# A new timetable for the Fourier jobs in a fused Fourier-filter and MLP kernel

## The chip, the cores and the metric

The kernel runs on one core of a Trainium2 chip. The metric is device time in microseconds of one execution. Before the change it is 1558.96 us, the median of three runs (1558.42 to 1561.44). All data are 32-bit floats.

The core has a matrix engine (TensorE, in the profile PE, with its weight loads apart as PEld), three engines for elementwise work (VectorE as DVE, ScalarE as ACT, GpSimd as POOL), a queue engine (SyncE as SP), and 16 DMA engines that they share. DMA transfers are issued from SP, ACT and POOL, each in the order of its own instructions.

## The reference

Two blocks follow each other. The first is a filter in the Fourier space of the sequence, for eight sequences (batch) of 3136 rows and 256 channels:

```python
X = np.fft.rfft(x, axis=1)                      # x: (8, 3136, 256)
Y = X * (filt_r + 1j * filt_i)[None, :, :]
y = np.fft.irfft(Y, n=x.shape[1], axis=1)
```

The second takes the 25088 rows of the result as tokens:

```python
h = y.reshape(25088, 256) @ w_in                # 256 -> 1024
e = np.exp(h - h.max(-1, keepdims=True))
solu = h * (e / (e.sum(-1, keepdims=True) + 1e-9))
ln = (solu - mean(solu)) / np.sqrt(var(solu) + 1e-6) * g_ln
out = ln @ w_out                                # 1024 -> 256
```

## The kernel before

**Tokens.** The 25088 tokens are 196 blocks of 128. The main loop has 196 + 9 steps `k`; block k gets its hidden layer in step k, and later steps finish it. Two blocks form a pair, and a pair's work spans an even step and the odd one after it, so "pair j" below is steps 2j and 2j + 1. From pair 3 on each pair's first layer is seven products (line 875, tile `m`) instead of eight, in Strassen's manner, and its second layer seven projections (line 1022, tile `o`). The sums of operands that this needs are GpSimd's (line 854: four short ones of `y` for the first layer, and four of 128x512 each, tiles `u` and `solu_t`, for the second). ScalarE does the exponential (920), the square for the variance (940) and copies out of PSUM (896, 1038); VectorE the maxima (907, 910), the normalisation (932), a 32x32 block transpose (950) and the rest of the output (1042). SP regroups the transposed blocks by DMA (967, into `solu_t`) and stores the output (1050).

**Fourier jobs.** A sequence of 3136 = 49 x 64 rows is transformed in two stages with one trip through DRAM between them (`d1`), and back in two stages with another (`d2`). For each sequence e there are:

- 8 *first steps* (F): load rows of x on SP (line 273), a difference on VectorE (282) and a sum on GpSimd (288), eight matmuls of 49 rows (297, tile `pa`), two ScalarE copies (302), two stores to `d1` from the POOL queue (308).
- 7 *spectra* (S): load of `d1` (320) and of a table (835) from the ACT queue and of the filter (784) from the POOL queue, sixteen matmuls of 64 rows (330, tile `pb`), then the complex product on VectorE (353 to 355; line 355 is the addition of the two parts, with both inputs in SBUF). The seventh unit of a sequence is smaller than the other six.
- 7 *inverses* (I), always one step after their spectrum: sixteen matmuls of 64 rows (330, tile `pc`), two copies on ScalarE (406), a store to `d2` from the POOL queue (412), in the step after that.
- 8 *steps back* (B): two loads of `d2` from the POOL queue (421), 64 short matmuls of 50 rows (437, tile `py`), a ScalarE copy (442), two VectorE operations that write `y` (450, 451).

So F4 is a first step of sequence 4, and so on. The ordinary matmuls of the pair (875, 1022) use 128 rows; those of the four jobs use a half of the array's rows.

**What sets their places.** `PLAN` (line 41) has for each sequence e three lists of steps: of its first steps, of its spectra, and of its steps back. The loop at line 1066 puts each job's parts into lists by step: a spectrum at step t puts its matmuls into `early[t]`, its inverse into `late[t + 1]`, its stores into `stores[t + 2]`; a first step goes to `late[t]`; a step back to `early[t]` (a second one for the same step to `late[t]`). Function `step` (1146) runs these lists at fixed points among the pair's own operations: `early` after product 2 of an even step or products 5 of an odd one, `late` at the end of the step. In a step where both are planned, a step back's matmuls stand directly before the spectrum's, and an inverse's directly before the first step's:

```python
            for job in early[k]:          # line 1202
                job()
...
        for job in late[k] + loads[k]:    # line 1292
            job()
```

Loads of rows (for F, and of `d2` for B) have four buffers; line 1134 gives each load its step: three steps ahead of its use, or as soon as the load four places earlier has been used. The spectrum's loads are issued one pair ahead (lists `spectrum_loads` and `loads`). The order on every engine's queue is the order of the program; nothing is moved later.

Which jobs share a pair is thus a matter of `PLAN` alone. Before the change the plan of a sequence from e = 4 on repeats every 24 steps (12 pairs), and in steps 78 to 101, for example, pairs 39 and 40 have a step back each, 41 and 42 a step back, a spectrum and an inverse, 43 to 45 all four jobs, 46 and 47 all but a step back, 48 and 49 a first step, and pair 50 a first step and a step back.

Of the kernel before, what the change touches and what calls it, by code (L numbers as in the profile page):

```python
# [37 lines left out]
DIRECT = 3  # L38


PLAN = [
    None,
    ([0] * 6 + [1] * 2, [4, 5, 6, 7, 8, 10, 12], [16, 17, 18, 19, 20, 20, 21, 22]),
    ([3, 4, 5, 6, 7, 8, 9, 10], range(18, 32, 2), [34, 36, 38, 40, 42, 44, 46, 46]),
    ([15, 23, 25, 27, 29, 31, 33, 35], range(38, 52, 2), range(54, 70, 2)),
    (range(39, 55, 2), range(58, 72, 2), range(76, 92, 2)),
    (range(63, 79, 2), range(82, 96, 2), range(100, 116, 2)),
    (range(87, 103, 2), range(106, 120, 2), range(126, 142, 2)),
    (range(111, 127, 2), range(130, 144, 2), range(150, 166, 2)),
]  # L50
EPS_LN, EPS_SM = 1e-6, 1e-9

# [58 lines left out]
def kernel(  # L111
# [954 lines left out]
    for e in range(1, B):  # L1066
        first_at, spectrum_at, back_at = PLAN[e]
        sp = Spectrum(e, pools, load_filter, load_de)
# [269 lines left out]
```

## Time and profile before

| | |
|---|---|
| median of three runs | 1558.96 us |
| the profiled execution | 1558.44 us |
| its span, first to last instruction | 1556.7 us |
| PE, PEld busy | 1534.5 us (99%), 1066.0 us (68%) |
| DVE, POOL, ACT busy | 1241.3 us (80%), 1107.3 us (71%), 923.3 us (59%) |
| granted TensorE clock | 0.997 of full speed |
| DMA | 297.58 MB, mean 191 GB/s |

The columns of the profile: in the table of stages each row is a stretch of the span from:to in us, its length, then for each engine its busy time and the number of its instructions, the granted clock, the mean busy share of the 16 DMA engines and what they moved in GB/s. In the timeline each row is a start, a duration, an engine (PEld: a weight load), a line, an operation, the tile written and those read, shapes, and how many were merged into the row; in brackets stands how long the engine sat idle before it and what ended that. Matmuls are pipelined and their ends are modelled, so that the start of the next weight load says more than a matmul's end. A pair's start is here the start of its first product of line 875; there are fourteen matmuls of that line to a pair.

### The profile page before, as it was taken

What the parts mean: (1) busy time and instruction counts of PE and PEld (TensorE: products, weight loads), DVE (VectorE), ACT (ScalarE), POOL (GpSimd) and SP (SyncE); (2) the same over time, 40 slices, a digit from 0 to 9 for tenths busy, and PEclk for the clock granted to TensorE, in tenths of its full rate; (3) what the DMA queues carried; (4) which work ended last, traced back from release to release, by engine and by line L of the source; (5) the groups of instructions that cost most, each with busy time, mean ns of one, the idle gap of its engine ahead of it and who ended that gap; (6) DMA issues with size and microseconds to landing.
All of it is one profiled execution on the core that took longest, in us unless ns stands there. A gap on an engine that the chain in (4) does not pass through costs nothing. (4 is left out here: it accounts for less than half of the span.)

```text
span 1556.7 us, 36704 instructions
## 1 busy us (share of the span) xinstructions
PE 1534.5 (99%) x12922; PEld 1066.0 (68%) x12922; DVE 1241.3 (80%) x2220; ACT 923.3 (59%) x1893; POOL 1107.3 (71%) x1290
## 2 busy tenths in 40 slices
PE   9999999999999999999999999999999999999997
PEld 6735676666666776667666776667676777777777
DVE  5888878988988798868897699877987777777772
ACT  4556565665556565665656555665656656666662
POOL 2226776797879776986689678996767766676665
PEclk9999999999999999999999999999999999999999
DMA  9779587867986788667886678766874544344444
GB/s 250 267 254 274 160 229 218 238 196 212 245 242 188 188 247 238 198 164 202 248 230 183 166 209 246 209 181 185 228 206 118 135 122 121 97 119 105 107 109 109
DMA packets 340831, 297.58 MB, mean 191 GB/s; under 512 B 27313, under 2 KB 310731, under 8 KB 340649
## 3 DMA queue, kind: packets, MB, share of 16 engines
q1 hardware_dynamic: 277864, 175.33, 42.4%
q0 software_dynamic: 29152, 87.33, 18.7%
q10 hardware_dynamic: 33634, 32.58, 7.1%
q8 instruction: 105, 1.72, 0.5%
q14 instruction: 76, 0.62, 0.1%
HBM read 117.53 MB, written 74.84 MB: 124 GB/s over the span
## 5 line engine op out<-in xcount | busy, mean ns | idle before, releaser
L1022 PEld LDWEIGHTS o<-w_out_sb,solu_t 128*128 128x128 f32 x3136 | 381.7, 192 | 49.9 <-issue 43.1
L1022 PE MATMUL o<-w_out_sb,solu_t 128*128 128x128 f32 x3136 | 401.3, 276 | 3.7 <-DVE ot L1042 3.1
L1022 PEld LDWEIGHTS o<-w_out_sb,u 128*128 128x128 f32 x2352 | 307.3, 192 | 138.3 <-issue 108.6
L875 PE MATMUL m<-w_in_sb,s 128*128 128x512 f32 x760 | 384.5, 607 | 2.4 <-ACT h L896 1.6
L1022 PE MATMUL o<-w_out_sb,u 128*128 128x128 f32 x2352 | 310.7, 276 | 2.3 <-POOL u L854 1.8
L932 DVE SCALAR_TENSOR_TENSOR h<-e,h 128x1024 f32<-128x1024 f32 x196 | 304.5, 1554 | 0.0
L875 PE MATMUL m<-w_in_sb,y 128*128 128x512 f32 x570 | 297.1, 603 | 1.7 <-DVE h L907 1.2
L1038 ACT ACTIVATE ot<-o,rs_t 128x128 f32<-128x128 f32 x392 | 143.2, 367 | 244.6 <-PE o L1022 242.8
L896 ACT COPY h<-m 128x512 f32<-128x512 f32 x285 | 167.7, 588 | 200.5 <-PE m L875 179.7
L854 POOL TENSOR_TENSOR u<-solu_t 128x512 f32<-128x512 f32 x98 | 135.2, 1380 | 186.7 <-DMA solu_t<-turn 131.0
L910 DVE CUSTOM_DVE_ANT_0 h<-m,h 128x512 f32<-128x512 f32 x190 | 130.1, 685 | 166.8 <-ACT h L896 104.0
L940 ACT ACTIVATE h<-h,nmu 128x1024 f32<-128x1024 f32 x196 | 224.9, 1147 | 41.8 <-DVE turn L950 41.7
L950 DVE STREAM_TRANSPOSE turn<-h 128x1024 f32<-128x1024 f32 x196 | 243.2, 1241 | 3.2
L920 ACT ACTIVATE e<-h,nmax 128x1024 f32<-128x1024 f32 x196 | 225.3, 1149 | 9.3 <-DVE h L932 7.9
L854 POOL TENSOR_TENSOR u<-solu_t,u 128x512 f32<-128x512 f32 x98 | 136.9, 1396 | 99.6 <-PE o L1022 99.3
L1042 DVE SCALAR_TENSOR_TENSOR ot<-o,rs_t,ot 128x128 f32<-128x128 f32 x299 | 103.8, 347 | 100.1 <-ACT ot L1038 61.4
L875 PEld LDWEIGHTS m<-w_in_sb,s 128*128 128x128 f32 x760 | 124.5, 191 | 80.3 <-issue 63.0
L854 POOL TENSOR_TENSOR u<-u,solu_t 128x512 f32<-128x512 f32 x98 | 162.6, 1659 | 16.8 <-PE o L1022 7.6
L854 POOL TENSOR_TENSOR solu_t<-solu_t,solu_t 128x512 f32<-128x512 f32 x98 | 155.6, 1587 | 0.9
L875 PEld LDWEIGHTS m<-w_in_sb,y 128*128 128x128 f32 x570 | 93.6, 190 | 89.6 <-issue 45.9
L854 POOL TENSOR_TENSOR s<-y 128x128 f32<-128x128 f32 x190 | 94.4, 497 | 0.5
L437 PEld LDWEIGHTS py<-wb_t,t 50*64 50x64 f32 x3584 | 57.6, 134 | 42.9 <-issue 19.4
(153 smaller groups left out, 1939.0 us busy)
## 6 DMA issues: line engine op xcount, KB each, us to landing
solu_t<-turn SPq DMA_DIRECT2D x780, 128.0 KB
out_dram<-ot SPq DMA_DIRECT2D x196, 128.0 KB
t<-d POOLq DMA_DIRECT2D x112, 200.0 KB, 6.7
t<-d ACTq DMA_DIRECT2D x37, 512.0 KB
f<-f_dram POOLq DMA_DIRECT2D x37, 512.0 KB, 7.9
d<-g POOLq DMA_DIRECT2D x36, 512.0 KB, 4.8
d<-x POOLq DMA_DIRECT2D x80, 200.0 KB, 5.2
de<-de_tbl ACTq DMA_DIRECT2D x37, 256.0 KB
```

The source lines that it names most:

```text
L437: nc.tensor.matmul(out=views[g][64 * h:64 * h + 64, cb, i, :], lhsT=t4[rows, i, c0:c0 + 64], rhs=wb_t[rows, 0:N1], start=True, stop=True)
L854: nc.gpsimd.tensor_tensor(out=out, in0=in0, in1=in1, op=op)
L875: nc.tensor.matmul(out=ms[j, bank], lhsT=lhsT, rhs=w_in_sb[:, w, :], start=m in (1, 2, 7), stop=True, skip_group_check=True)
L896: nc.scalar.copy(out=h_half(k, i), in_=ms[j, 0])
L910: nc.vector.tensor_tensor_reduce(out=h_half(k, i), in0=ms[j, bank], in1=h_half(*kept), scale=1.0, scalar=sofar, op0=ALU.add, op1=ALU.min, ...
L920: nc.scalar.activation(out=e, in_=hs[k], func=AFT.Exp, bias=nmaxs.pop(k)[:, 1:2], scale=-1.0, accum_out=esums[g][:, i:i + 1])
L932: nc.vector.scalar_tensor_tensor(out=solu, in0=e, scalar=SHRINK, in1=solu, op0=ALU.mult, op1=ALU.mult, accum_out=nmu)
L940: nc.scalar.activation(out=solu, in_=solu, func=AFT.Square, bias=nmu, scale=-float(DFF), accum_out=variances[g][:, i:i + 1])
L950: nc.vector.transpose(out=turns[g][:, :, i, :], in_=solus[k].rearrange("p (f j) -> p f j", j=32))
L1022: nc.tensor.matmul(out=pos[p, bank], lhsT=lhs[:, f, :], rhs=w[:, f, :], start=f == 0 and (m in (1, 2, 7) or alone), stop=True, skip_group_ ...
L1038: nc.scalar.activation(out=out_half(p, *to)[0], in_=pos[p, 0], func=AFT.Copy, scale=rs)
L1042: nc.vector.scalar_tensor_tensor(out=ot, in0=pos[p, bank], scalar=rs, in1=out_half(p, *kept)[0], op0=ALU.mult, op1=ALU.add)
```

## The change

Only `PLAN` changes, with a small function that writes a list of seven steps with gaps. Spectra and steps back of a stretch of 24 steps from t now go to steps t, t+2, t+6, t+8, t+12, t+14, t+16 (and the eighth step back to t+18), and the first steps of the next sequence to the odd steps after those. From step 52 on the pattern of a stretch is: two pairs with all four jobs, one with none, two with all four, one with none, three with all four, one with a step back and a first step, two with none. In the stretch from 124 there is no sequence left for first steps. The steps before 52 are arranged anew as well: the spectra of sequence 2 begin at 14 instead of 18, the first steps of sequences 3 and 4 come earlier, the second step back that stood at 46 goes to step 35. Sequence 1 and the steps back of sequence 7 (150 to 164) stay where they were. No operation, tile or buffer is added or removed.

```diff
+def beside(t):
+
+    return [t + i for i in (0, 2, 6, 8, 12, 14, 16)]
+
+
 PLAN = [
     None,
     ([0] * 6 + [1] * 2, [4, 5, 6, 7, 8, 10, 12], [16, 17, 18, 19, 20, 20, 21, 22]),
-    ([3, 4, 5, 6, 7, 8, 9, 10], range(18, 32, 2), [34, 36, 38, 40, 42, 44, 46, 46]),
-    ([15, 23, 25, 27, 29, 31, 33, 35], range(38, 52, 2), range(54, 70, 2)),
-    (range(39, 55, 2), range(58, 72, 2), range(76, 92, 2)),
-    (range(63, 79, 2), range(82, 96, 2), range(100, 116, 2)),
-    (range(87, 103, 2), range(106, 120, 2), range(126, 142, 2)),
-    (range(111, 127, 2), range(130, 144, 2), range(150, 166, 2)),
+    ([3, 4, 5, 6, 7, 8, 9, 10], [14, 16, 22, 24, 26, 28, 30], [34, 35, 36, 38, 40, 42, 44, 46]),
+    ([13, 15, 17, 23, 25, 27, 29, 31], range(36, 50, 2), beside(52) + [70]),
+    (range(33, 49, 2), beside(52), beside(76) + [94]),
+    ([t + 1 for t in beside(52)] + [71], beside(76), beside(100) + [118]),
+    ([t + 1 for t in beside(76)] + [95], beside(100), beside(124) + [142]),
+    ([t + 1 for t in beside(100)] + [119], beside(124), range(150, 166, 2)),
 ]
```

## The prediction, made before the changed kernel ran

> **What bounds the kernel now.** I read the page first: shares, then chain. TensorE is busy all through, at full clock (0.997), and the chain that ended last goes through its products and projections.
>
> ```profile
> PE 1534.5 (99%) x12922; PEld 1066.0 (68%) x12922; DVE 1241.3 (80%) x2220; ACT 923.3 (59%) x1893; POOL 1107.3 (71%) x1290
> ...
> PE 38%; DMA 1%; POOL 0%; issue 0%; SPq 0%; ACTq 0%; DVE 0%; POOLq 0%; ACT 0%
> ```
>
> The change moves no operation into or out of the kernel, so an average over the span can't price it. I therefore cut the span at the starts of the pairs (each fourteenth matmul of line 875) and asked for busy times by stage. The rows are pairs 86 (no job), 76 (B), 48 (F), 50 (B and F), 54 (B, S, I), 46 (S, I, F), 32 (all four), 45 and 22 (all four); all have an even j except 45.
>
> ```profile
> core 0: us, PE busy (x) PEld busy (x) DVE busy (x) ACT busy (x) POOL busy (x), PEclk, DMA share, GB/s
> 1367.16:1379.64 12.48, 12.48 (x74) 9.13 (x73) 9.11 (x18) 7.70 (x17) 8.48 (x10) 1.00 0.44 118
> 1234.39:1248.15 13.76, 13.76 (x138) 10.08 (x137) 9.38 (x20) 8.20 (x18) 8.96 (x11) 1.00 0.52 142
> 824.25:837.93 13.68, 13.68 (x82) 9.40 (x80) 10.23 (x21) 8.93 (x19) 12.45 (x15) 1.00 0.64 176
> 851.40:866.36 14.96, 14.96 (x148) 10.35 (x144) 12.57 (x23) 9.43 (x20) 12.68 (x15) 1.00 0.68 172
> 909.37:925.31 15.94, 15.94 (x173) 11.30 (x169) 15.23 (x26) 9.51 (x20) 10.83 (x13) 1.00 0.81 236
> 793.75:809.57 15.82, 15.82 (x116) 10.60 (x112) 15.17 (x27) 10.00 (x23) 13.20 (x15) 1.00 0.76 215
> 576.46:593.25 16.79, 16.79 (x181) 11.62 (x177) 14.41 (x27) 10.26 (x22) 12.69 (x15) 1.00 0.90 259
> 775.88:793.75 17.87, 16.83 (x179) 11.47 (x175) 16.58 (x25) 9.68 (x21) 13.63 (x17) 1.00 0.83 232
> 418.89:437.49 18.60, 17.03 (x179) 11.69 (x177) 15.74 (x29) 10.77 (x25) 13.01 (x17) 1.00 0.97 268
> ```
>
> Seven rows have PE busy for the whole stretch: the pair takes what TensorE takes. The prices of the jobs follow by subtraction. B alone is 13.76 - 12.48 = 1.28, F alone 13.68 - 12.48 = 1.20, both in one pair 2.48: they add up, since one stands in the even step and the other at the end of the odd one. But with all four jobs, F costs 16.79 - 15.94 = **0.85** and B 16.79 - 15.82 = **0.97**. So F next to an inverse is 0.35 us cheaper, and B next to a spectrum 0.31. Spectrum and inverse have the rest, 16.79 - 12.48 - 0.85 - 0.97 = 2.49. (Odd pairs start from 12.27, without the small matmul that even ones have for the deviations; a sequence's last, smaller spectrum and inverse cost 13.82 - 12.27 = 1.55 in pair 71.) Why, the weight loads of pair 32 show:
>
> ```profile
> 578.20 0.30 PEld L875 LDWEIGHTS m<-w_in_sb,y 128*128 128x128 f32 x2
> 579.26 1.02 PEld L437 LDWEIGHTS py<-wb_t,t 50*64 50x64 f32 x64 [0.76 <-issue]
> 580.19 0.69 PEld L330 LDWEIGHTS pb<-t,de 64*64 64x64 f32 x16
> 581.27 0.30 PEld L875 LDWEIGHTS m<-w_in_sb,s 128*128 128x128 f32 x2 [0.39 <-issue]
> ```
>
> Going from 128-row matmuls to half-row ones opens a gap of 0.76 us in which no weights are loaded, going back one of 0.39 (0.82 after a first step); from `py` to `pb` there is none. Two neighbouring jobs share one way in and one way out.
>
> **The change by parts.** *Neighbours gained.* From the lists of the plan: F stands directly behind an inverse 5 + 7 + 5 + 5 + 5 = 27 times before (sequences 3 to 7) and 8 + 6 + 7 + 7 + 7 = 35 after; B directly ahead of a spectrum 3 + 5 + 6 + 5 + 5 + 6 = 30 times before (sequences 1 to 6) and 2 + 6 + 7 + 7 + 7 + 7 = 36 after. (The second B of step 46, now at 35, is alone in both.) That is 8 x 0.35 + 6 x 0.31 = **-4.7 us** on TensorE, on the path since nothing else ends these pairs. As a check I added such prices for every pair from 12 to 95: outside the pairs named next, and pair 14 (0.4 over), the sum meets the measured pair within 0.13 us.
>
> *Losses in full pairs.* Beyond its TensorE time, 16.57 (odd j) or 16.79 (even), a pair with all four jobs sometimes takes longer. The fifteen such pairs of before and their losses: pairs 19 to 23 0.6, 0, 0.8, 1.8, 0.6; 31 to 34 none; 43 to 45 0, 0, 1.3; 55 to 57 0.8, 0, 0. Together 5.9 us, 0.39 a pair. The new plan has 27 of them: 18 to 23, then seven in each of three stretches. Two causes are seen. In pair 45 a VectorE addition of two tiles in SBUF (line 355, median 0.855) ran 3.33 us while two GpSimd sums ran one behind the other, the output's VectorE operation came late, and the projection waited 1.23 us for its bank:
>
> ```profile
> 783.61 3.33 DVE L355 TENSOR_TENSOR pr<-pr,pt 128x512 f32<-128x512 f32 x1
> 783.88 1.27 POOL L854 TENSOR_TENSOR solu_t<-solu_t,solu_t 128x512 f32<-128x512 f32 x1
> 785.11 1.27 POOL L854 TENSOR_TENSOR u<-solu_t,u 128x512 f32<-128x512 f32 x1
> 787.25 0.97 PEld L1022 LDWEIGHTS o<-w_out_sb,solu_t 128*128 128x128 f32 x8 [1.23 <-DVE ot L1042]
> ```
>
> In pair 22, the fourth full one in a row, DMA is at 0.97 of its capacity, rows of x land late and ScalarE stands 4.25 us, partly behind its own DMA issues:
>
> ```profile
> 430.88 0.69 DVE L282 TENSOR_TENSOR diff<-x 113x512 f32<-113x512 f32 x1 [1.84 <-DMA x<-in_x_dram]
> 431.18 0.58 ACT L896 COPY h<-m 128x512 f32<-128x512 f32 x1 [4.25 <-DMA x<-in_x_dram]
> ```
>
> Bounds for the new losses: all gone, -5.9; or all 27 like pairs 19 to 23 (3.8 / 5 = 0.76), 27 x 0.76 - 5.9 = +14.6. I go by the place in a row of full pairs. First ones lost 1.4 in four, second ones 0 in four, third ones 2.1 in four, later ones 2.4 in three. The new plan has 10 firsts, 10 seconds, 4 thirds and 3 later ones: 3.6 + 0 + 2.1 + 2.4 = 8.1, so +2.2. But a first pair now follows an empty one, in which DMA is at 0.44 and GpSimd has no stores of earlier jobs to issue; half the firsts' loss is nearer. I take **+0.6**.
>
> *Other pairs.* Pairs 8 to 11 lost 0.1, 0.6, 1.4, 0.2 (pair 10 had two B in one step, S, a third B and I), 24 lost 0.9. The new pair 8 has B and S, then B, F and I: TensorE 18.1 us by the prices, VectorE some 17; no row shows this mix. Between no loss and pair 10's 1.4 I take 1.0, the mix being close to that one; pairs 9 and 10 have no spectrum any more, so 9 to 11 are put at 0.5 together; 24, left with a small S and I, at 0.1. That is 1.6 where 3.2 was, with bounds -3.2 (nothing lost) and +3.3 (8 to 11 at 1.4 each, 24 at its 0.9). Against these -1.6 I set one more loss like pair 22's 1.8 in the row 18 to 23, since pair 17 ahead of it now has two B and an F: **+0.2**.
>
> *What else moves with a job.* Each F takes along its loads on SP (among the regroupings of line 967), a VectorE difference (0.91), a GpSimd sum (1.29) and two stores on POOL (0.53 each); S two loads on the ACT queue, a load (0.75) and a store (0.78) on POOL, six VectorE operations (about 4.7 us), two ScalarE copies (0.56 each); B two POOL loads (0.54 each), a ScalarE copy (0.48), two VectorE operations (0.55 each). A full pair holds the same set before and after: VectorE 14.4 of 16.8 us, GpSimd 12.7, ScalarE 10.3. That cover is what hides them; where it fails is the loss above. Loads keep their lead in steps, but an empty pair is 12.4 us instead of 13.8: a spectrum's loads, issued 7 us into the pair before, have 9 us until the first `pb`, and pair 52's, landing 4 us after issue at a low DMA share, show room. Waits of the POOL queue on `d2` (B at 52, loaded at the end of the step that stores the last inverse) are as before at 54.
>
> Sum: -4.7 + 0.6 + 0.2 = -3.9. Against the profiled execution of 1558.44 (span 1556.7 and 1.7 around it; 0.5 below the median of the runs) this gives **1554.5 us**.
>
> **The rivals.**
> - *Loss by the number of full pairs* (VectorE and GpSimd in each other's way in each). At the old mean, 27 x 0.39 - 5.9 = +4.6 eats the gain: 1558.4. For: full pairs put the additions of line 355 beside the sums in each. Against: eleven of fifteen lost at most 0.6.
> - *Slower: every full pair like pairs 19 to 23*, through the same place, line 355 behind two GpSimd sums. 27 x 0.76 - 5.9 - 4.7 gives about +10: 1568.4. It decides above 0.51 a pair, (4.7 + 5.9 + 3.1) / 27, where 3.1 us is 0.2%, about what a measurement of this kernel can tell from no change. Against: pairs 31 to 34, four in a row without any loss.
> - *A longer first row.* Pairs 18 to 23 are six in a row behind a laden pair 17, where five lost 3.8, the last two 2.4 of it. DMA backlog adds two more such at 1.2 to 1.8, +3: about 1557.5.
> - *Empty pairs clear the queues*: the losses of the later stretches vanish (-2.1 instead of +0.6) and the first row gains a little: 1551.
>
> [...]
>
> **How the numbers follow.** My forecast has 0.45 (its own range 1552.5 to 1556.5), the empty-pair gain 0.10, the longer first row 0.10, loss by number 0.17, the slower rival 0.18. Faster by over 0.2% (under 1555.3) is most of the forecast, 0.38, and the gain: 0.48. Within 0.2%: 0.05 of the forecast, the first row, most of loss by number: 0.30. Slower: 0.22 with the tails. The range 1550.5 to 1562.5 leaves out the upper part of the slower rival and little below.
>
> **What would show it.** Pairs with all four jobs from 26 on at 16.57 and 16.79 us, empty ones at 12.27 and 12.48, pair 35 at 14.75; the same 0.76 gap, fewer of them (14 fewer ways in). Wrong if line 355 is long (over 2.5 us) in more than four or five full pairs, if empty pairs take over 12.6, since work left behind by a full pair holds TensorE there, or if spectra wait for `t`.

## The result, and the profile after

The changed kernel takes 1572.67 us (median of six runs, 1565.29 to 1576.64) against 1558.69 for the kernel before (six runs on the same chip, 1557.54 to 1563.36): a ratio over all runs of 1.0082 [1.0056, 1.0108] (the quotient of the two medians is 1.0090), so it is slower by 13 to 14 us where 4 us less were forecast. The profiled execution took 1572.86 us, its span 1571.1, at a granted clock of 0.998. (Line numbers of the changed kernel are 5 higher: 355 is now 360, 282 is 287, 437 is 442.)

The page of the changed kernel, engines and chain:

```profile
PE 1535.5 (98%) x12922; PEld 1065.1 (68%) x12922; DVE 1235.9 (79%) x2220; ACT 922.4 (59%) x1893; POOL 1098.0 (70%) x1290
...
PE 23%; DMA 1%; DVE 1%; issue 0%; POOL 0%; SPq 0%; ACT 0%; ACTq 0%; POOLq 0%; DVEq 0%
```

Busy shares have hardly moved; nothing in them tells of 14 us. The stages do. Cut at the pairs as before, the rows are pairs 86 (no job), 35 (B and F), 38 and 39 (a first and a second full pair), 40 (the empty one behind them), 26 (the first full pair of the new pattern), then 41, 42 and 43 (first full, second full, empty):

```profile
core 0: us, PE busy (x) PEld busy (x) DVE busy (x) ACT busy (x) POOL busy (x), PEclk, DMA share, GB/s
1382.90:1395.39 12.49, 12.49 (x74) 9.14 (x73) 8.88 (x18) 7.71 (x17) 8.55 (x10) 1.00 0.43 116
642.75:657.49 14.74, 14.74 (x144) 10.12 (x142) 10.87 (x21) 9.07 (x18) 11.23 (x15) 1.00 0.56 153
682.36:699.05 16.69, 16.69 (x178) 11.53 (x176) 14.72 (x27) 9.63 (x21) 10.76 (x10) 1.00 0.86 244
699.05:715.61 16.56, 16.56 (x178) 11.39 (x174) 14.82 (x27) 10.11 (x21) 16.12 (x18) 1.00 0.71 199
715.61:728.35 12.74, 12.74 (x77) 9.16 (x73) 10.97 (x18) 8.48 (x19) 10.26 (x14) 1.00 0.81 234
492.36:514.07 21.71, 18.71 (x179) 12.45 (x177) 14.95 (x27) 9.76 (x21) 10.11 (x11) 0.92 0.81 219
728.35:746.03 17.68, 17.68 (x176) 11.64 (x174) 15.71 (x25) 8.74 (x18) 11.99 (x14) 1.00 0.88 232
746.03:763.59 17.56, 17.56 (x179) 12.05 (x177) 15.87 (x27) 10.13 (x22) 15.00 (x16) 1.00 0.64 184
763.59:777.03 13.44, 12.87 (x72) 8.85 (x71) 9.72 (x20) 9.25 (x21) 9.33 (x14) 1.00 0.78 204
```

Two things stand in these rows. Where nothing is late, the pairs have the forecast lengths (16.69, 16.56, 14.74, 12.49). And the empty pair 40, between full ones, has DMA at 0.81, not at the 0.43 of an empty pair far from any job: the loads of the full pairs that follow are issued in it. In pairs 26 and 41 to 43 together 4.9 + 1.1 + 0.8 + 1.2 us are lost.

From here on the *loss* of a pair is its length less what the prediction's TensorE prices give for its jobs. Summed over pairs 4 to 96, the prices are 4.7 us lower after the change; the losses rise from 13.4 to 34.7 us, by 21.4 (21.35 before rounding); the stretches ahead of pair 4 and behind pair 96 are 2.3 us shorter: -4.7 + 21.4 - 2.3 = 14.4, which is the difference of the spans, 1571.1 - 1556.7.

Four kinds of place hold the new losses. The waits of VectorE's difference and of the steps back, after the change and before it (total us, times, longest):

```profile
DVE diff L287 <- DMA x<-in_x_dram: 21.2, 11, 3.3
...
PE py L442 <- DMA t<-d: 4.6, 4, 2.5
...
PEld py L442 <- DMA t<-d: 4.0, 2, 3.3
```

```profile
DVE diff L282 <- DMA x<-in_x_dram: 3.0, 4, 1.8
```

In the timeline of the changed kernel they look like this (pair 26, pair 29, pair 57):

```profile
497.63 0.20 PEld L442 LDWEIGHTS py<-wb_t,t 50*64 50x64 f32 x4 [3.32 <-DMA t<-d]
...
553.25 0.58 ACT L901 COPY h<-m 128x512 f32<-128x512 f32 x1 [2.90 <-DMA x<-in_x_dram]
553.61 1.64 DVE L287 TENSOR_TENSOR diff<-x 113x512 f32<-113x512 f32 x1 [2.23 <-DMA x<-in_x_dram]
...
987.13 0.69 DVE L287 TENSOR_TENSOR diff<-x 113x512 f32<-113x512 f32 x1 [3.30 <-DMA x<-in_x_dram]
988.49 0.30 PEld L880 LDWEIGHTS m<-w_in_sb,y 128*128 128x128 f32 x2 [3.16 <-DVE nmax L915]
```

(1) In pair 26 the first step back waits for its own load. (2) In pairs 20, 29, 32 and 57 the difference stands at the head of VectorE's queue without its rows; behind it are the maxima, and in pair 57 TensorE's next product waits until they are read (the last row). (3) In the second of two full pairs, 30 and again 42, VectorE's addition of the imaginary part is long, and the inverse's products of that part (tile `pc` from `pi`) have to wait for it:

```profile
574.74 2.50 DVE L360 TENSOR_TENSOR pi<-pi,pt 128x512 f32<-128x512 f32 x1
575.40 1.28 POOL L859 TENSOR_TENSOR u<-solu_t 128x512 f32<-128x512 f32 x1
...
576.50 0.63 PEld L335 LDWEIGHTS pc<-pr,de 64*64 64x64 f32 x8
...
576.76 1.62 POOL L859 TENSOR_TENSOR u<-u,solu_t 128x512 f32<-128x512 f32 x1
...
577.29 0.20 PEld L335 LDWEIGHTS pc<-pi,de 64*64 64x64 f32 x4 [0.16 <-DVE pi L360]
...
579.17 0.30 PEld L880 LDWEIGHTS m<-w_in_sb,y 128*128 128x128 f32 x2 [0.82 <-DVE h L912]
```

In a pair without loss, here 38, the weights of the two parts are loaded by turns:

```profile
697.15 0.14 PEld L335 LDWEIGHTS pc<-pr,de 64*64 64x64 f32 x2
697.18 0.14 PEld L335 LDWEIGHTS pc<-pi,de 64*64 64x64 f32 x2
```

In pair 30 the eight loads of the real part go first and alone. From the inverse's first weight load to the start of the next pair it takes 1.91 us in pair 38 and 2.67 in pair 30, and that is the pair's loss; the gap of 0.82 in the last row is the ordinary one behind a first step. This meeting costs 0.77 us in the full pair and 1.18 in the empty one, the same within 0.02 us in both places; pair 63 (B, S and I) loses 1.29 beside an addition of 2.26 us.

The first full pairs 29 and 41 have a meeting too. The difference has waited for its rows, so GpSimd's sum of the same rows falls beside the addition of the imaginary part (2.33 us in both pairs); the stretch from the inverse to the next pair is 2.86 us there, 0.95 over pair 38's. A late transfer and a long addition are thus not always two separate causes:

```profile
557.36 2.33 DVE L360 TENSOR_TENSOR pi<-pi,pt 128x512 f32<-128x512 f32 x1
...
557.85 1.27 POOL L293 TENSOR_TENSOR x<-x 113x512 f32<-113x512 f32 x1
```

(4) The rows of sequences 2 and 3, pairs 4 to 25, lose 16.0 us where they lost 10.9; 1.6 of the difference is in pair 4, whose plan is the same in both.

### The profile page after: what moved, and what is told of

It reads as the page before. It is cut to its first block, busy times and chain, and to the rows that moved or that the text cites. A ratio compares the mean times of both kernels' runs of the same rounds, so it can differ in the third digit from the quotient of the medians.

```text
span 1571.1 us, 36679 instructions
## 1 busy us (share of the span) xinstructions
PE 1535.5 (98%) x12922; PEld 1065.1 (68%) x12922; DVE 1235.9 (79%) x2220; ACT 922.4 (59%) x1893; POOL 1098.0 (70%) x1290
## 3 DMA queue, kind: packets, MB, share of 16 engines
q0 software_dynamic: 29152, 87.33, 18.4%
## 5 line engine op out<-in xcount | busy, mean ns | idle before, releaser
L937 DVE SCALAR_TENSOR_TENSOR h<-e,h 128x1024 f32<-128x1024 f32 x196 | 291.7, 1488 | 0.0
L859 POOL TENSOR_TENSOR u<-solu_t 128x512 f32<-128x512 f32 x98 | 131.5, 1341 | 194.3 <-DMA solu_t<-turn 102.2
L859 POOL TENSOR_TENSOR u<-u,solu_t 128x512 f32<-128x512 f32 x98 | 157.4, 1606 | 18.8 <-PE o L1027 12.5
L442 PEld LDWEIGHTS py<-wb_t,t 50*64 50x64 f32 x3584 | 58.4, 134 | 48.6 <-PE o L1027 14.4
```

The source lines that it names most:

```text
L442: nc.tensor.matmul(out=views[g][64 * h:64 * h + 64, cb, i, :], lhsT=t4[rows, i, c0:c0 + 64], rhs=wb_t[rows, 0:N1], start=True, stop=True)
L859: nc.gpsimd.tensor_tensor(out=out, in0=in0, in1=in1, op=op)
L937: nc.vector.scalar_tensor_tensor(out=solu, in0=e, scalar=SHRINK, in1=solu, op0=ALU.mult, op1=ALU.mult, accum_out=nmu)
```

## The experiments

Two theories stood against each other. *Transfers*: rows and tables land later than their lead allows, and VectorE, which is 14.7 to 15.9 us busy in the full pairs shown above, can't make up for it. *VectorE*: its additions of line 360, lengthened beside GpSimd's sums, are the loss, and the transfers are only what is seen in front. Each kernel was compared with the kernel before on the same chip, whose median there was 1558.97, 1560.95, 1560.84, 1560.89 and 1560.65 us; so ratios are compared, not times.

**Transfers left out of the new plan**

```diff
 def load_filter(sp, u, ...):        # and load_de in the same way
+    if sp.e > 3 or sp.e == 3 and u > 1:
+        return kept_f[u % 2]
```

> The changed kernel, with less DMA: from sequence 3's third unit on, the spectra use the filter and table tiles of that sequence's first two units again instead of loading their own, so 33 of 37 pairs of such loads (512 and 256 KB, some 25 of 297.6 MB) are left out and the output is not the reference's. Theory D (transfers land late: VectorE waited 21.2 us for rows of x at its difference instead of 3.0, TensorE waited for rows of the step back): most of the loss goes, 0.994 to 1.000 of the kernel before. Theory V (VectorE and GpSimd block each other at the addition of line 360): nothing changes, 1.006 to 1.010.

1562.23 us (ten runs), 1.0014 [0.9994, 1.0033]. The waits of the difference for x fall from 21.2 us to 1.5, pair 26 loses 1.4 us in place of 4.9, and the row from 18 to 24 no longer loses anything. The meeting of pairs 42 and 43 stays as it was:

```profile
730.16:747.70 17.54, 17.54 (x180) 12.05 (x177) 15.53 (x25) 9.23 (x19) 11.31 (x14) 1.00 0.54 159
747.70:761.14 13.44, 12.86 (x72) 8.84 (x71) 9.73 (x20) 9.26 (x21) 9.09 (x14) 1.00 0.73 199
```

**Additions left out of the new plan**

```diff
-            add(out=out, in0=out, in1=term, op=(ALU.subtract, ALU.add)[part])
+            if self.e < 2:
+                add(out=out, in0=out, in1=term, op=(ALU.subtract, ALU.add)[part])
```

> The changed kernel without the addition that ends each part of the complex product (line 360) from sequence 2 on, so each product has only one of its two terms. TensorE, ScalarE, GpSimd and DMA do the same work. Theory V: the loss goes, 0.994 to 1.000 of the kernel before. Theory D: VectorE gets some slack to make up for late rows, but waits as long for them; 1.003 to 1.008.

1559.45 us (ten runs), 1.0003 [0.9982, 1.0024]. The rows of x are as late as before (21.2 us of waits, 14 times), but from pair 38 on they cost nothing. Pairs 42 and 43 have the forecast lengths:

```profile
742.64:759.42 16.78, 16.78 (x180) 11.62 (x176) 12.36 (x23) 10.44 (x23) 13.95 (x16) 1.00 0.67 197
759.42:771.79 12.37, 12.37 (x75) 9.02 (x71) 7.73 (x18) 7.97 (x17) 9.20 (x14) 1.00 0.81 227
```

With either part left out the new plan is level with the whole kernel before. Without controls that says little, since leaving work out can help the old plan too.

**The controls, and both parts left out at once**

> Edit: the old plan, with the filter and the de tiles of the first two jobs of sequence 3 used again by every later job, so 33 of the 37 later loads of each kind are not made (the results of sequences 3 on are then not the reference's). It is the control of after_light. Theory D (late transfers, which the new plan alone makes dear) expects little here: the losses of the old plan in pairs 26 on sum to about 2 us, so 1555 to 1559 us, and the TensorE gain of 4.7 us then shows as after_light minus before_light only where the new plan's remaining losses are taken off. If fewer transfers help the old plan as much as they helped the new one (10 us), the loss of the new plan is not its own, and the time would be about 1549 us.

> Edit: the old plan without the addition of line 355 from sequence 2 on (the results of sequences 2 on are then not the reference's). It is the control of after_noadd, which took 1559.5 us. Theory V (VectorE has no room to catch up in a full pair of the new plan) expects little here, since the old plan has losses of 3.2 us only in pairs 45 and 55 and of about 4 us in its first row: 1553 to 1558 us. If the old plan gains as much as the new one (13 us), then the addition is dear in both plans and explains nothing of the change: about 1546 us.

> Edit: the new plan with both cuts, the loads left out as in before_light and the addition left out as in before_noadd (the results of sequences 2 on are then not the reference's). If late transfers and a full VectorE together are the whole of the loss, hardly any loss is left from pair 26 on, and the new plan shows its TensorE gain: 4.7 us less than before_both, 1549 to 1553 us. If a third cause is at work (order of the jobs on the tensor engine's own queue, rows of the first sequences), more than 5 us of loss stays behind pair 13 and the time is above 1555 us.

> Edit: the old plan with both cuts (the results of sequences 2 on are then not the reference's). Control of after_both: 1554 to 1557 us if the old plan lost little to either cause; the ratio after_both to before_both is expected at 0.997, 4.7 us, if the gain on the tensor engine is real and the rest of the loss is named.

| | old plan | new plan |
|---|---|---|
| nothing left out | 1558.69 us | 1572.67 us, 1.0082 [1.0056, 1.0108] |
| loads left out | 1553.37 us, 0.9949 [0.9929, 0.9969] | 1562.23 us, 1.0014 [0.9994, 1.0033] |
| additions left out | 1555.69 us, 0.9972 [0.9959, 0.9986] | 1559.45 us, 1.0003 [0.9982, 1.0024] |
| both left out | 1551.31 us, 0.9940 [0.9919, 0.9960] | 1548.74 us, 0.9927 [0.9905, 0.9948] |

The change costs +0.82% as it is, +0.65% without the loads, +0.31% without the additions, and -0.13% without both. With both left out there are 2.6 us between the two medians, on one chip, where 4.7 were expected; the runs overlap (1547.36 to 1550.45 and 1549.17 to 1551.52 us), so the sign alone is likely, not its size. The loads helped the old plan nearly as much as the new one (5.1 against 6.8 thousandths), which the transfer theory had not expected; the additions helped the new plan three times as much (7.9 against 2.8). The losses by stretch say where. Each row is one execution only, and the last column tells how far it lies from the median of its kernel. The column before it is the part of the sum that comes from stretches at half the granted clock behind a stall (half of their length, an estimate that takes TensorE to be busy all through them; the last section shows some):

| loss in us, pairs | 4 to 25 | 26 to 37 | 38 to 96 | sum | at half clock | execution less median |
|---|---|---|---|---|---|---|
| old plan | 10.9 | 0.0 | 2.5 | 13.4 | 0 | -0.3 |
| old, loads out | 7.8 | -0.1 | 1.6 | 9.3 | 0 | +0.3 |
| old, additions out | 8.8 | 0.0 | 1.4 | 10.2 | 0 | +0.2 |
| old, both out | 6.5 | -0.1 | -0.1 | 6.3 | 1.7 | -0.2 |
| new plan | 16.0 | 9.8 | 8.9 | 34.7 | 1.7 | +0.2 |
| new, loads out | 8.3 | 3.3 | 6.8 | 18.4 | 0 | -5.7 |
| new, additions out | 13.4 | 10.0 | 0.5 | 23.9 | 6.8 | +3.0 |
| new, both out | 9.8 | 0.9 | -0.1 | 10.7 | 0 | +1.7 |

Up to pair 37 the loads carry more of the loss: without them it falls by 14.2 us, without the additions by 2.4. But 6.8 us of the latter execution, all ahead of pair 38, and 1.7 of the new plan's are at half clock; with these taken off the two numbers are 12.5 and 7.6, and the first comes from an execution well below its median. From pair 38 on, where none of these is at half clock, it is the additions: without them the loss falls by 8.4, without the loads by 2.1. With both out nothing is left from pair 38 on. Ahead of pair 26 3.3 us over the old plan remain (5.0 with the half clock taken off) and eat most of the gain; what they come from these kernels don't show.

**Loads issued earlier** (two steps more lead)

```diff
-        at = max(t - 3, earliest, ...
+        at = max(t - 5, earliest, ...
```

> The changed kernel with rows of x and of the steps back loaded up to five steps ahead of their use instead of three, as far as the four buffers allow: the same transfers, earlier. If D is a matter of too short a lead in the short empty pairs: 0.995 to 1.002 of the kernel before. If D is a matter of how many bytes fall into one stretch, or if V holds: 1.006 to 1.010.

1570.05 us (four runs), 1.0077 [1.0049, 1.0105], in the range expected if the bytes of a stretch or the additions set the loss. The waits for x do fall, and pairs 27 on lose 6 us in place of about 14; but the early rows lose more, pair 26 among them:

```profile
DVE diff L287 <- DMA x<-in_x_dram: 5.0, 3, 3.5
```

```profile
500.15:523.08 22.93, 19.92 (x178) 13.62 (x177) 15.03 (x27) 9.75 (x21) 12.16 (x14) 0.85 0.80 211
```

So the longer lead did not bring the time down: what it gave from pair 27 on was lost again in the rows ahead (23.2 us in pairs 4 to 25, 16.0 without the longer lead; 6.1 in place of 4.9 in pair 26). Of these, 5.1 and 3.4 us are at half clock, and this execution is the slowest of the four, 5.5 us above their median. That an earlier load takes the place of another where transfers are dense would explain the rest, and is not shown.

**Parts of the change.** New only from step 76 on; new only ahead of step 52; all but the stretch from 52 to 75; and all up to 75. The edits are rows of `PLAN`, for the first two:

```diff
 # new from step 76 on
-    (range(33, 49, 2), beside(52), beside(76) + [94]),
-    ([t + 1 for t in beside(52)] + [71], beside(76), beside(100) + [118]),
+    (range(39, 55, 2), range(58, 72, 2), beside(76) + [94]),
+    (range(57, 73, 2), beside(76), beside(100) + [118]),
 # new ahead of 52
-    (range(33, 49, 2), beside(52), beside(76) + [94]),
+    (range(33, 49, 2), range(58, 72, 2), range(76, 92, 2)),
```

> The new plan from step 76 on, the old one ahead of it: sequences 1 to 3 as before, sequence 4 with its old first steps and spectra, sequence 5 with first steps at 57 to 71. In the traces the starts of pairs of the changed kernel run 5.1 us behind those of the kernel before at pair 26, 13.9 at pair 38, 14.3 at pair 50 and 15.0 at pair 62, so the regular stretches from 76 on lose about as much as they gain. If the place decides (the crowded first half): 0.998 to 1.001 of the kernel before. If the pattern of two full pairs and an empty one loses wherever it stands: 1.003 to 1.006.

> Edit: the new plan of the sequences up to step 53 alone (first steps of sequence 2 at 14 to 30, of sequence 3 at 36 to 48 and of sequence 4 at 33 to 47) and the old plan of everything behind it. It is the other half of the run with the new plan from step 76 on, which came out at 1.003. If the loss sits in the first rows (the old plan's back-to-back transfers of sequences 2 and 3, and the steps back at 52), this half is slower by 5 us or more, 1563 to 1568 us. If it sits in the repeated block of two full pairs and an empty one, it is within 2 us of before.

> Edit: the new plan ahead of step 52 and from step 76 on, with the old plan's steps in between (steps back of sequence 3 at 54 to 68, spectra of sequence 4 at 58 to 70, first steps of sequence 5 at 57 to 71). By the two halves measured before (1.0013 for the steps ahead of 52, 1.003 from 76 on) it should be at 1.004, 1566 to 1568 us, if losses add up. By the trace of the whole new plan, which loses 9.6 us in pairs 26 to 35 for about 1 us of gain there, leaving this stretch out gives 1572.7 - 8.6 = 1564 us. If a row of full pairs is dear only through the backlog that it hands on, the losses ahead of and behind the stretch shrink too and the time is below 1562 us.

> Edit: the new plan up to step 75 and the old plan from step 76 on. The complement of the run that was new from step 76 on alone (1.003). If losses add up: the whole new plan's 1.0082 less 0.003, 1.005, 1567 to 1570 us. By the trace, in which pairs 38 on lose 5.3 us more than before for 3.3 us of gain, 1570 to 1572 us. If the stretch from 52 to 75 is dear only with the new plan on both sides, below 1565 us.

From 76 on alone: 1561.63 us, 1.0030 [1.0011, 1.0048]. Ahead of 52 alone: 1563.35, 1.0013 [0.9998, 1.0027]. All but 52 to 75: 1569.48, 1.0068 [1.0043, 1.0094]. All up to 75: 1571.67, 1.0076 [1.0051, 1.0101]. (In the second expectation the lists "at 14 to 30" and "36 to 48" are spectra, not first steps.) So no part is a gain, and the regular pattern loses even where the old plan stands ahead of it. The ratios don't simply add up: the stretch from 76 on costs 3.0 thousandths behind the old plan, 5.5 behind the new early rows (1.0068 - 1.0013), and 0.6 behind both other parts. But the intervals of the two last kernels are 0.0025 either way, so adding up isn't refuted, and which expectation for them is right can't be said. Backlog handed from one stretch to the next would make parts reinforce each other; it isn't shown, and the profile of "all up to 75" speaks against much of it, since the old plan from pair 38 on loses 3.2 us there, 2.5 in the old kernel (one execution, 5.4 us below its median).

**The step back at 52**

```diff
-    ([13, 15, 17, ..., 31], range(36, 50, 2), beside(52) + [70]),
+    ([13, 15, 17, ..., 31], range(36, 50, 2), [54, 58, 60, 62, 64, 66, 68, 70]),
```

> Edit: the new plan with the steps back of sequence 3 at 54, 58, 60 and so on to 70 in place of 52, 54, 58 and so on to 68 and 70, so that the table loaded for the first of them no longer has to land at the start of pair 26. The theory that pair 26 waits for this table expects its 4.9 us of loss to go to under 1.5 and nothing else to move: 1567 to 1570 us. If the row of full pairs is short of VectorE and of transfers whatever the first of them waits for, the loss moves to the pairs behind it (27 to 32) and the time stays at 1571 to 1574 us.

1571.28 us (seven runs, 1564.49 to 1575.55), 1.0068 [1.0045, 1.0092]. (What the expectation calls a table are the rows of `d2`.) Pair 26, now without a step back, takes what its jobs cost:

```profile
489.43:505.29 15.86, 15.86 (x115) 10.43 (x113) 14.32 (x25) 8.85 (x20) 10.09 (x10) 1.00 0.96 253
```

With the wait the loss of that pair is gone, as expected, in an execution that is the fastest of the seven; but the ratio fell by only 0.0014, about 2 us, well within its interval, so whether part of the loss moved behind it stays undecided. The same plan with the loads five steps ahead from step 53 on, and the plan that is new from 76 on with this lead:

> Edit: as the run with the first step back at 54, and the loads of rows are issued up to five steps ahead in place of three from step 53 on. Late transfers as the theory expect the waits of the differences for x rows to fall from 21 us to about 5 and the losses from pair 27 on from 13 us to about 5: 1558 to 1564 us. [...]

> Edit: the new plan from step 76 on and the old one ahead of it, with the loads of rows up to five steps ahead from step 53 on. It is meant to keep the gain on the tensor engine of the later sequences (3.3 us) without the losses of the first rows and without late x rows. Theory: 1556 to 1560 us, 1 to 4 us below the run without the earlier loads; if the loads five steps ahead crowd other transfers, as they did in pairs 18 to 26, it is above 1563 us.

The first took 1568.01 us, 1.0044 [1.0025, 1.0062]. The kernel before was 2.2 us slower on this chip than in the result above; with that taken off, 1565.9 lies above the 1558 to 1564 us expected of late transfers. The waits for x did fall to 4.8 us; in its profile, 4.4 us above the median, pair 53 alone lost 6.4 us, 3.4 of it at half clock. The second took 1561.30 us, 1.0001 [0.9979, 1.0022]: no gain over the kernel before. In both the longer lead, given only from step 53 on, goes with a ratio 2.4 to 2.9 thousandths below that of the same plan without it (1.0068 and 1.0030), the way that the transfer theory expected; the intervals overlap, so this is likely and not shown.

**The addition moved to GpSimd**, so that nothing is left out. The condition reaches sequence 2 as well, as in the kernel without additions:

```diff
+            if part == 1 and self.e > 1:      # part == 0 in the third kernel below
+                add = nc.gpsimd.tensor_tensor
             add(out=out, in0=out, in1=term, op=(ALU.subtract, ALU.add)[part])
```

> Edit: the new plan with the second addition of each spectrum product (the sum of the imaginary part, line 360 for part 1) made by GpSimd in place of VectorE from sequence 3 on. Nothing is left out. Leaving both additions out of sequences 3 on gave 1559.5 us against 1572.7. If what counts is that VectorE has no free time in a full pair and is held up beside GpSimd's sums, VectorE is relieved of 0.86 to 2.5 us per full pair: 1561 to 1567 us. If GpSimd, 16.5 of 17 us busy in some second full pairs, has no room for another 1.3 us, its sums come later and the outputs behind them wait: 1572 us or more.

> Edit: the same move of the second addition to GpSimd in the old plan. Nothing is left out. Leaving both additions out gave 0.9972 here. VectorE theory: 1556 to 1560 us, at best 2 us below before. If GpSimd has no room: above 1560 us.

> Edit: the new plan with the first addition of each spectrum product (the real part, line 360 for part 0) made by GpSimd in place of VectorE from sequence 3 on. Nothing is left out. The second addition was the one seen at 2.50 us beside two early GpSimd sums; if that meeting is the main loss, moving the first addition does little, 1569 to 1574 us. If VectorE's room is what counts, whichever operation is taken off, it gives about the same as moving the second: within 3 us of that run.

> Edit: the plan that is new from step 76 on and old ahead of it, with the second addition made by GpSimd from sequence 3 on. Nothing is left out. That plan alone gave 1.003, with about 5 us of loss where the addition meets two sums and 3.3 us of gain. VectorE theory: 1555 to 1559 us, at or below before. If GpSimd has no room: above 1562 us.

1606.61 us, 1.0296 [1.0269, 1.0322] with the new plan; 1585.24, 1.0168 [1.0149, 1.0186] with the old one; 1595.92, 1.0234 [1.0198, 1.0270] with the plan that is new from 76 on. The waits of the first of them show why: the addition stands in GpSimd's queue between sums, and the inverse waits for it. Of the 60.5 us of loss in its pairs 4 to 96, 13.7 are at half clock:

```profile
PEld pc L335 <- POOL pi L362: 21.8, 11, 4.5
PE pc L335 <- POOL pi L362: 17.4, 7, 4.0
```

With the first addition, the real part, moved instead: 1570.84 us, 1.0080 [1.0050, 1.0110], the same as without the move. VectorE's busy time falls from 1235.9 to 1216.5 us, and pairs 42 and 43 have their forecast lengths in the profile; but GpSimd has 1.25 us more per spectrum, and the losses are 16.2, 7.5 and 7.6 us in the three stretches, as large as without the move. So the time lies where the expectation about the meeting put it, but not for its reason: this meeting went, and other losses came, in other pairs (29 loses 3.4 us, 45 2.1). VectorE's relief at GpSimd's cost gave nothing here; what VectorE's work alone is worth, without its meetings, these kernels don't tell apart.

No kernel of these that computes everything was faster than the one before.

## Why the prediction was wrong

**Neighbours gained, -4.7 us: right.** TensorE goes over from 128-row to half-row weights 121 times in place of 135 behind the first pairs, the 14 fewer that the plan said, and where nothing is late the pairs are within 0.1 us of 16.57, 16.79 and 14.75. Pair 38's weight loads show the same gaps as pair 32's did:

```profile
685.08 1.02 PEld L442 LDWEIGHTS py<-wb_t,t 50*64 50x64 f32 x64 [0.76 <-PE o L1027]
686.00 0.69 PEld L335 LDWEIGHTS pb<-t,de 64*64 64x64 f32 x16
687.08 0.30 PEld L880 LDWEIGHTS m<-w_in_sb,s 128*128 128x128 f32 x2 [0.39 <-issue]
```

**Losses in full pairs, +0.6: the step that failed.** The 27 full pairs lose 18.8 us against 5.9 before, so +12.9. By their place: first ones 9.8 in ten, where the forecast halved 3.6; second ones 4.1 in ten, where it had 0; thirds 1.9 (2.1), later ones 3.0 (2.4). So the two classes grew that the new pattern makes many of. "A first pair now follows an empty one, in which DMA is at 0.44" took the row of pair 86, which has no successor with jobs; the empty pairs directly ahead of a full one have 0.66 to 0.86, and the first full pair begins with the backlog: 4.9 of the 9.8 us are pair 26's wait for its step back and what followed it, 1.8, 1.1 and 1.0 stand in pairs 29, 41 and 32 behind late rows of x. "Second ones 0" came from four pairs, each ahead of a third full one. Of the six second ones that now have an empty pair behind them, 30 and 42 meet two GpSimd sums under their last addition and lose 0.77 each (54 does so too when the loads are left out); 2.6 us are the late rows of pair 57.

**Other pairs, +0.2: failed too.** They gave the remaining +8.5. The pairs counted, 8 to 11 and 24, lost 3.2 us, twice the 1.6 put down, and others were not counted as able to lose: 31 and 43 with 1.2 each behind the meeting, 63, 69 and 90 with 1.3, 0.7 and 0.5. Pairs 4 to 17 lose 3.4 more than before in all, half of it in pair 4, where no job was moved.

**What else moves with a job, 0.** The leads were argued for the spectra's loads, and these were on time: no product of line 335 waits for a transfer in the profile, and of the products with the filter one, for 1.1 us, in the first sequences. The rows of x and of `d2` were not looked at, although the plan moves them into the same empty pair; the time from their last issue to the difference is 8.1 us on average before and 8.6 after, and with the waits taken off 8.1 in both, so it isn't the lead that got shorter but the landing that got later. The step back at 52 was called "as before at 54", which holds in steps; but the pair between its load and its use is now an empty one of 12.4 us, and the load landed 3.3 us late.

**The rivals.** The time is nearest to that of the slower rival, 1568.4, and its 0.76 us per full pair is close to the 0.70 measured. Its place is half right. In the full pairs line 360 is over 2.3 us four times (29, 30, 41, 42) and at most 2.50, so the sign "over 2.5 us in more than four or five" failed; in those of the kernel before it was so four times as well (19, 21, 45, 55), so long additions in full pairs have not become more, and what is new lies in what follows them and in the late rows. The total of the imaginary additions on VectorE grew by 7 us, of which the meetings are a part, that of the real ones by 0.7:

```profile
L355 DVE TENSOR_TENSOR pi<-pi,pt 128x512 f32<-128x512 f32 (+1 forms) x43 | 37.2, 864 | 1.5
```

```profile
L360 DVE TENSOR_TENSOR pi<-pi,pt 128x512 f32<-128x512 f32 (+1 forms) x43 | 44.0, 1023 | 1.5
```

"Empty pairs clear the queues" is refuted by their DMA share (0.66 to 0.86). Of the other signs named, the empty pairs over 12.6 us (31, 40, 43, 52) came true.

**The long additions.** In pair 30 the addition took 2.50 us; in pair 26 one with no GpSimd sum beside it (at 502.40 us) took 0.69. That and one sum of 1.28 make 2.0, an estimate of what waiting for a whole sum would give: the order of size agrees. The order of the two doesn't: by the profile the addition began 0.66 us ahead of the first sum (574.74 and 575.40). Why it took 2.50 us is not shown. Additions of over 2.3 us stand in four of the 21 full pairs from 26 on.

## What to carry to other kernels

Here a plan that took 4.7 us off the bounding engine by bunching work lost 21.4 us more beside it; with the loads and the additions left out of both plans the losses differ by 4.4 (10.7 and 6.3, one execution each). The mean load did not tell this (VectorE was 80% busy before and 79% after), and neither did a quiet stretch with no bunch behind it (DMA 0.43 in pair 86, 0.81 in pair 40). Read the load of the stretch ahead of a bunch from one that has the same successor, or count the loads that will be issued in it. Where two relieves each help, run both, each with its control on the old kernel: only then does one see which of them belongs to the change. And put the granted clock beside losses that are read from one execution each: here it made up an estimated 6.8 of 23.9 us in one of them and nothing in others.

## What was not expected of the hardware

Here a stall cost more than its length: pair 26, with a wait of 3.32 us, lost 4.9. Behind the wait the granted clock was at half (0.50) for 3.41 us, shown in stretches of the changed kernel's span:

```profile
497.60:499.89 2.29, 1.75 (x74) 1.63 (x78) 0.81 (x2) 0.33 (x1) 1.93 (x1) 1.00 0.90 234
499.89:503.30 3.41, 3.41 (x17) 1.62 (x10) 2.93 (x5) 1.48 (x4) 0.00 (x0) 0.50 0.55 162
503.30:506.00 2.70, 2.70 (x20) 2.22 (x20) 0.65 (x2) 0.93 (x3) 1.74 (x2) 1.00 0.47 120
```

By that clock the work of these 3.41 us would take 1.7 at full speed, an estimate, so 1.7 of the pair's 4.9 us of loss. Ahead of the stretch the weight loads stood for 3.32 us and the matmuls for 2.49. In pair 57 they stood for 3.16 and 2.33, and the granted clock was 1.00 from 984 to 1002 us. What halved the clock behind the one wait and not behind the other is not shown. In the kernel without additions pair 26 ran at a mean clock of 0.85 and pair 32 at 0.92, by the same estimate 3.4 + 1.7 us of their 9.8 us of loss:

```profile
490.14:512.56 22.42, 20.07 (x178) 13.81 (x176) 13.77 (x27) 10.02 (x22) 10.11 (x11) 0.85 0.77 207
587.26:608.25 20.99, 18.58 (x179) 12.25 (x177) 13.93 (x27) 9.92 (x22) 10.18 (x14) 0.92 0.87 228
```

Left open: why the rows of x land later in the new plan although DMA is no busier in its full pairs (0.64 to 0.95) than in those of the old one (0.74 to 0.97), and how one stretch's backlog acts on the next.
